# Windowed attention and feed-forward layer: half of the weight halves on GpSimd, the first token tile split straight from PSUM, the weight decode moved to later steps

## The chip, the cores and the metric

The kernel runs on one core of a Trainium2 chip. The metric is the device time of one execution in microseconds (us), as the median of several executions. A profiled execution gives the trace that is read below: the busy times of the engines TensorE (PE, with its weight loads as PEld), VectorE (DVE), ScalarE (ACT) and GpSimd (POOL), and of the DMA queue that SyncE (SP) issues.

## The reference

The kernel computes attention for 8 batches of 8 heads, with 512 local and 32 global tokens of 64 values each. A global token sees every token; a local token sees the 32 global tokens and the local ones within 32 places. The result, as 4352 rows of 512 values, goes through a feed-forward layer whose weights are given in 64 bit.

```python
s_g = scale * np.matmul(q_g, k_all.transpose(0, 1, 3, 2))
out_g = np.matmul(sm(s_g), v_all)
mask = np.abs(pos[:, None] - pos[None, :]) <= window          # window = 32
s_l = np.concatenate([s_lg, np.where(mask, s_ll, -1e9)], axis=-1)
out_l = np.matmul(sm(s_l), np.concatenate([v_g, v_l], axis=2))
...
h = x @ w_in            # (4352, 512) @ (512, 2048)
r = np.maximum(h, 0.0)
g = s * (r * r) + b
return (g @ w_out).astype(np.float32)
```

## The kernel before

**Steps.** One loop runs over steps j. Step j below 128 handles one slot of attention: batch, half of 256 queries, and head, in that order, so that eight steps fill one tile of 256 tokens by 512 values. Feed-forward unit m follows ten steps behind (LAG = 10): unit m works on tile t = m // 8 and on two of the 16 pieces of the hidden layer. It multiplies the tile with its two pieces of w_in (`ffn_in`, 24 matmuls, L517), squares and scales (L523 to L533), and one step later multiplies with two pieces of w_out (`ffn_out`, 12 matmuls, L549). Units 0 to 7 work on tile 0 and so need chunks 0 and 1, then 2 and 3, up to 14 and 15 of the weights, in steps 10 to 17.

**Precision.** Every operand of a fast matmul is split into a high half in the fp32r format and a low half, value minus high half; three products stand for one. The first 16 steps (NF = 16, tiles 0 and 1 of the tokens) instead use plain float32 matmuls for attention, which need no split of keys, queries and values.

**Weights.** A chunk holds 128 x 512 values of w_in and of w_out, each of 64 bits, 1 MB in all. `weight_load` brings it into a staging tile of the place that SPOTS names: xs0 or xs1 (the places that later hold the split token tiles) or one of two kq places (later the split keys and queries). `weight_chunk` decodes it in two halves, w_in first (`at.start` 0) and then w_out (`at.start` 512), in `weight_words`: two ACT operations (L160, L161), a shift and a sum on DVE (L164, L165), the high half on ACT (L168) and the low half on DVE (L169). DECODED_AT gives the step at which the decode of each chunk is issued in program order, here chunk k in step k; its load is issued two steps earlier.

**Token tiles.** In float32 steps `pv32` writes, at every odd head, a block of 128 x 256 values from PSUM to the tile x, with a DVE copy for the first eight steps (L349) and an ACT copy later (L347). One step after a tile is complete, `x_split` makes its high halves on ACT (L489) and its low halves on DVE (L490), two blocks of 128 x 512 each. SPLIT_AT names those steps: tile 0 in step 9.

**Order of the engines' queues.** The program order gives priorities only. A planner orders the instructions of every engine by priority, with a model of their durations, and an instruction is placed where its inputs and its place in memory are free in that model. Attention of the first 16 steps is given a priority 50 places earlier than its position (AHEAD = 50). On the chip every engine runs its own queue strictly in the planned order.

Of the kernel before, what the change touches and what calls it, by code (L numbers as in the profile page):

```python
# [23 lines left out]
HALF = 256  # L24
# [23 lines left out]
SPLIT_AT = {8 * t + 9: t for t in range(16)}  # L48
# [1 line left out]
WARM_FIRST = 20  # L50
WARM_HEAD = 4

SPOTS = ["xs0", "xs1", "kq", "kq"] * 2 + ["xs1", "kq", "kq"] * 2 + ["xs1", "kq"]
DECODED_AT = list(range(16))
BY_HALVES = 16
NORM_ACT = lambda j: j < 0
X_ACT = lambda j: j >= 8
# [8 lines left out]
def f32(ap):  # L66
    return ap.bitcast(F32)
# [3 lines left out]
def window_attention_then_ffn(ctx: ExitStack, tc: tile.TileContext, qd, qg, kw, vw, vg, qz, qgz, vz, w_in, w_out, sv, bv, out):  # L71
    nc = tc.nc
# [37 lines left out]
    for tile_, c0, shift in ((mask_low, 32, -32), (mask_mid, 32, 0), (mask_high, 0, 32)):  # L110
        nc.gpsimd.memset(tile_, 0.0)
        part = tile_[:, c0:c0 + 192]
        for sign, base in ((1, -shift), (-1, 64 + shift)):
            nc.gpsimd.affine_select(
                out=part, in_=part, pattern=[[sign, 192]], compare_op=ALU.is_ge,
# [16 lines left out]
    def split_tile(tag, name, shape, bufs):  # L132
        n = math.prod(shape)
        whole = ops.tile([P, n], F32R, tag=tag, name=name, bufs=bufs)
        return whole[:, 0:n].rearrange("p (a b c) -> p a b c", a=shape[0], b=shape[1])
# [3 lines left out]
    def weight_load(k):  # L139
        st = ops.tile([P, 2048], I32, tag=SPOTS[k], name=f"wst{k}", bufs=1 + (SPOTS[k] == "kq"))  # L140
        staged[k] = st
        sources = (w_in[k], w_out[k * P:(k + 1) * P, :])
        for i in range(2):
            queue = nc.scalar if k == 0 else nc.sync
            queue.dma_start(st[:, 1024 * i:1024 * (i + 1)], sources[i])

    def weight_chunk(k):
        st = staged.pop(k)
        n = 2 if k < BY_HALVES else 1
        for i in range(n):  # L150
            c = 1024 // n
            weight_words(k, st[:, 2 * c * i:2 * c * (i + 1)], slice(c * i, c * (i + 1)))

    def weight_words(k, st, at):
        words = st.rearrange("p (n w) -> p n w", w=2)
        low, high = words[:, :, 0], words[:, :, 1]
        n = at.stop - at.start
        pool, tag = ((ops, "vsg"), (sb, "pg"))[(k + at.start // 512) % 2]
        up = pool.tile([P, n], I32, tag=tag, name=f"wup{k}_{at.start}", bufs=1)
        nc.scalar.activation(out=up, in_=low.bitcast(U32), func=AF.Copy, scale=2.0**-29)  # L160
        nc.scalar.activation(  # L161
            out=low.bitcast(F32), in_=high.bitcast(F32), func=AF.Prelu, scale=2.0**-112, alpha=2.0**32,
        )
        nc.vector.tensor_scalar(out=low, in0=low, scalar1=3, scalar2=None, op0=ALU.logical_shift_left)  # L164
        nc.vector.tensor_tensor(out=low, in0=low, in1=up, op=ALU.add)  # L165
        m = low.bitcast(F32)
        hi, lo = (w_all[:, i, k].rearrange("p w c -> p (w c)")[:, at] for i in range(2))
        nc.scalar.copy(out=hi, in_=m)  # L168
        nc.vector.tensor_sub(out=lo, in0=m, in1=f32(hi))  # L169


    NS = B * 2 * H
# [2 lines left out]
    def slot(j):  # L175
        return j // 16, (j // 8) % 2, j % 8
# [77 lines left out]
    def x_tile(j):  # L254
        b, hf, h = slot(j)
        t = 2 * b + hf
        if h == 0:
            xcur[t] = sb.tile([P, 4, HALF], F32, tag="x", name=f"x{t}", bufs=1)
        return xcur[t]
# [56 lines left out]
    def pieces(hf):  # L316
        q0 = MIDQ[hf][0]
        yield 0, P, slice(0, P), slice(0, P)
        yield 2, P, slice(NP - P, NP), slice(P, 2 * P)
        yield 1, MID, slice(P, NP - P), slice(q0, q0 + NP - 2 * P)  # L320
# [10 lines left out]

    def pv32(j):
        b, hf, h = slot(j)
        x = x_tile(j)
        if h % 2 == 0:
            return
        p_o = ps.tile([P, 2 * P], F32, tag="o", name=f"ps_o{j}")
        for i in (j - 1, j):
            pt, rv = st_.pop(("pt", i)), st_.pop(("rv", i))
            for c, n, o, q in pieces(hf):  # L340
                nc.tensor.matmul(
                    p_o[:, q], lhsT=rv[0:n, c * P:(c + 1) * P], rhs=pt[0:n, o],
                    start=(i < j and c == 0), stop=(i == j and c == 1),
                )
        x_out = x[:, h // 2, :]
        if X_ACT(j):
            nc.scalar.copy(out=x_out, in_=p_o)  # L347
        else:
            nc.vector.tensor_copy(out=x_out, in_=p_o)  # L349

    def qg_load(b):
        rqg = sb.tile([P, H * SG], F32, tag="xr", name=f"rqg{b}", bufs=1)
        nc.sync.dma_start(rqg, qgz[0] if b == 0 else qg[b])
        st_["rqg", b] = rqg

    def qg_load32(b):
        n = min(NF - 16 * b, H) * SG
        rqg = ops.tile([P, n], F32, tag="u", name=f"rqw{b}", bufs=1)
        nc.sync.dma_start(rqg, qgz[b, :, 0:n])
        st_["rqg", b] = rqg  # L360

    def qg_split(b):
        rqg = st_["rqg", b].rearrange("p (h q) -> p h q", h=H)
        qgs = ops.tile([P, H, 2, SG], F32R, tag="qgs", name=f"qgs{b}", bufs=1)
        nc.scalar.copy(out=qgs[:, :, 0, :], in_=rqg)
        nc.gpsimd.tensor_sub(out=qgs[:, :, 1, :], in0=rqg, in1=f32(qgs[:, :, 0, :]))
        st_["qgs", b] = qgs
# [48 lines left out]
    def transposes_and_pv(jt, jp):  # L416
        if NF <= jp < NS:
            pv_products(jp)
        if NF <= jt < NS:
            p_transposes(jt)  # L420
        if NF <= jp < NS:
            pv_sum(jp)
        if NF <= jt < NS:
            p_split(jt)
# [57 lines left out]
    xs_ = {}  # L482
# [25 lines left out]
    def ffn_in(m):  # L508
        t, pr = m // 8, m % 8
        xs = xs_[t]  # L510
        p_h = ps.tile([P, 2, HALF], F32, tag="h", name=f"ps_h{m}", bufs=2)
        for k in range(2):
            f = 2 * pr + k
            n = 0
            for c in range(4):
                for a, e in ((0, 0), (0, 1), (1, 0)):
                    nc.tensor.matmul(  # L517
                        p_h[:, k], lhsT=wi[:, a, f, c], rhs=xs[:, e, c, :],
                        start=(n == 0), stop=(n == 11),
                    )  # L520
                    n += 1
        r = sb.tile([P, 2, HALF], F32, tag="r", name=f"r{m}", bufs=2)
        nc.scalar.activation(out=r, in_=p_h, func=AF.Relu)  # L523
        nc.vector.scalar_tensor_tensor(out=r, in0=p_h, scalar=s_t, in1=r, op0=ALU.mult, op1=ALU.mult)  # L524
        g = split_tile("g", f"g{m}", [2, 2, HALF], 2)
        if GL_POOL(m):
            nc.vector.tensor_scalar_add(r, r, b_t)
            nc.scalar.copy(out=g[:, 0], in_=r)
            nc.gpsimd.tensor_sub(out=g[:, 1], in0=r, in1=f32(g[:, 0]))
        else:  # L530
            nc.scalar.activation(out=g[:, 0], in_=r, func=AF.Identity, bias=b_t)  # L531
            nc.vector.scalar_tensor_tensor(  # L532
                out=g[:, 1], in0=r, scalar=b_t, in1=f32(g[:, 0]), op0=ALU.add, op1=ALU.subtract,  # L533
            )
        gs_[m] = g
# [32 lines left out]
    for b in range(B):  # L568
        for g in range(2):
# [4 lines left out]
            for i in range(2):  # L574
                h = 4 * g + 2 * i
# [23 lines left out]
    for j in range(NM + LAG + 2):  # L599
        if j == 3:  # L600
            nc.sync.dma_start(s_t, sv.partition_broadcast(P))
            nc.sync.dma_start(b_t, bv.partition_broadcast(P))
        sp(j + 1)
        ld(j + 2)
        vl(j)
        while loaded < 16 and (loaded < 2 or DECODED_AT[loaded] <= j + 2):
            weight_load(loaded)
            loaded += 1
        while piece < 16 and DECODED_AT[piece] <= j:
            weight_chunk(piece)  # L610
            piece += 1
        if j < NS:
            b1 = j // 16 + 1
            if j == 14 and NF > 16:
                qg_load32(1)
            elif j % 16 == 14 and b1 < B:
                qg_load(b1)
            sc(j)
            if j == NF - 1 and NF % 16:
                if NF > 16:  # L620
                    qg_load(j // 16)
                qg_split(j // 16)
            if j % 16 == 15 and NF <= j + 1 < NS:
                qg_split(b1)
        if j in early:
            early.pop(j)()
        m = j - LAG if LAG <= j < NM + LAG else None
        if m is not None:
            ffn_in(m)
            if m == 8 * 15 + 7:  # L630
                xg_split(16)
        tr(j - 1)
        transposes_and_pv(j - 1, j - 2)
        vsp(j - 1)
        for fn in extra.pop(j, []):
            fn()
        pvs(j - 2)
        vl32(j)
        if j in SPLIT_AT:
            x_split(SPLIT_AT[j])  # L640
        if last is not None:
            ffn_out(last)
        last = m
        if j in late:
            late.pop(j)()
# [73 lines left out]
```

## Time and profile before

| | us |
|---|---|
| median of 3 runs (1012.87 to 1013.37) | 1012.92 |
| the profiled execution | 1013.71 |
| its span in the trace | 1011.9 |
| PE / DVE / ACT / POOL busy within the span | 996.1 / 809.4 / 707.6 / 289.4 |
| first and last low half of a weight (L169) starts at | 8.4 / 103.6 |

The engines run side by side, and an engine's share of the whole span is an average over two stages: the first hundred us, in which the weights are decoded beside the float32 attention and the first feed-forward units, and the rest, in which nothing is decoded. A busy time of PE includes matmuls whose ends are modelled, so a busy PE isn't a PE at its peak. The chain of waits tells, for every stretch, on which engine the work ran that released the next.

### The profile page before, as it was taken

To read this page: it belongs to the slowest core of one execution; us is meant where nothing else is said; L and a number is where in the kernel's file an instruction comes from. 1 tells how busy PE (TensorE), PEld (TensorE's weight loads), DVE (VectorE), ACT (ScalarE), POOL (GpSimd) and SP (SyncE) were. 2 spreads that over 40 slices of the span, in tenths; PEclk is the share of its full clock that TensorE was granted. 3 is DMA by queue.
4 is the path that set the end of the run, shared out by engine and by line. 5 is a ranking of instruction groups with operands and counts; after the bars stand their busy time and mean duration, and the time that the engine had idled before them with its cause. 6 is when DMAs were issued, how large, how long until landed. Compare 5 with 4: busy or idle time off the path is not lost.

```text
span 1011.9 us, 20076 instructions
## 1 busy us (share of the span) xinstructions
PE 996.1 (98%) x6946; PEld 906.9 (90%) x6948; DVE 809.4 (80%) x2111; ACT 707.6 (70%) x1817; POOL 289.4 (29%) x366
## 2 busy tenths in 40 slices
PE   9799999999999999999999999999999999999998
PEld 5599899999999999999999999999999999999887
DVE  6999879988789788888789779988799788964322
ACT  7999767868677667868677667867678667743222
POOL 1001433424244224424234223424234223401000
PEclk9999999999999999999999999999999999999999
DMA  9765312313122212313132112312132112101000
GB/s 327 266 229 182 98 48 63 108 34 96 47 88 69 65 48 62 97 42 90 47 99 69 54 59 62 97 42 87 44 104 70 53 55 65 62 1 49 23 22 21
DMA packets 63557, 82.05 MB, mean 81 GB/s; under 512 B 7648, under 2 KB 50656, under 8 KB 63456
## 3 DMA queue, kind: packets, MB, share of 16 engines
q1 hardware_dynamic: 63168, 79.72, 25.2%
q8 instruction: 55, 0.90, 0.4%
q10 hardware_dynamic: 288, 1.05, 0.3%
q14 instruction: 46, 0.38, 0.1%
HBM read 71.30 MB, written 9.44 MB: 80 GB/s over the span
## 4 chain that ended last, share of the span: by engine, by line
PE 91%; ACT 5%; DVE 2%; DMA 1%; issue 0%
PE ps_h L517 35%; PE acc L549 35%; PE ps_s L375 5%; PE ps_o L403 4%; PE turned L311 3%; PE turned L313 3%; PE ps_og L469 2%; PE ps_g L382 1%; PE warm L105 1%; DMA rk<-in_kw 1%; ACT wst L161 1%; ACT wup L160 1%; ACT w_all L168 1%; ACT sm L231 1%; PE turned L447 1%; PE ps_s L286 1%
## 5 line engine op out<-in xcount | busy, mean ns | idle before, releaser
L517 PE MATMUL ps_h<-xst,w_all 128*128 128x256 f32 x3264 | 437.5, 281 | 1.8 <-ACT xst L502 0.7
L549 PE MATMUL acc<-w_all,g 128*128 128x512 f32 x1632 | 422.0, 396 | 0.0
L517 PEld LDWEIGHTS ps_h<-xst,w_all 128*128 128x128 f32 x3264 | 407.6, 189 | 9.3 <-ACT xst L489 1.1
L549 PEld LDWEIGHTS acc<-w_all,g 128*128 128x128 f32 x1632 | 289.8, 188 | 49.8
L214 POOL TENSOR_TENSOR vs<-rv,vs 128x192 fp32r<-128x192 f32 x112 | 70.7, 631 | 291.0 <-ACT vs L213 289.9
L524 DVE SCALAR_TENSOR_TENSOR r<-ps_h,s_t,r 128x512 f32<-128x512 f32 x136 | 101.4, 746 | 53.7 <-ACT r L523 52.2
L231 ACT ACTIVATE sm<-sm,nm 128x224 f32<-128x224 f32 x256 | 121.5, 478 | 32.5 <-DVE nm L225 31.3
L206 POOL TENSOR_TENSOR kq<-rq,kq 128x256 fp32r<-128x256 f32 x112 | 92.8, 828 | 169.2 <-ACT kq L205 160.3
L532 DVE SCALAR_TENSOR_TENSOR g<-r,b_t,g 128x512 fp32r<-128x512 f32 x136 | 112.0, 824 | 35.6 <-ACT g L531 31.1
L531 ACT ACTIVATE g<-r,b_t 128x512 fp32r<-128x512 f32 x136 | 98.6, 725 | 52.0 <-DVE r L524 51.9
L523 ACT ACTIVATE r<-ps_h 128x512 f32<-128x512 f32 x136 | 81.3, 598 | 67.7 <-PE ps_h L517 58.4
L241 DVE TENSOR_SCALAR sm<-sm,nm 128x224 f32<-128x224 f32 x256 | 92.2, 402 | 3.9
L461 POOL TENSOR_TENSOR vsg<-rvg,vsg 128x320 fp32r<-128x320 f32 x64 | 56.9, 910 | 107.1 <-ACT vsg L460 107.1
L375 PE MATMUL ps_s<-kq 128*128 128x224 f32 x448 | 73.7, 275 | 2.3 <-DVE nm L225 2.3
L375 PEld LDWEIGHTS ps_s<-kq 128*128 128x128 f32 x448 | 67.3, 190 | 8.9 <-ACT pt L328 2.5
L392 ACT CAST pt<-turned 128x416 fp32r<-128x416 f32 x112 | 57.5, 514 | 23.5 <-PE turned L313 22.8
L393 DVE TENSOR_TENSOR pt<-turned,pt 128x416 fp32r<-128x416 f32 x112 | 65.4, 584 | 6.9 <-ACT pt L392 6.2
L386 ACT COPY tg<-ps_g 32x256 f32<-32x256 f32 (+1 forms) x112 | 42.2, 377 | 33.9 <-PE ps_g L382 31.4
L387 DVE TENSOR_TENSOR sg<-ps_g,tg 32x256 f32<-32x256 f32 (+1 forms) x112 | 48.2, 430 | 20.7 <-ACT tg L386 15.9
L311 PE MATMUL turned<-ident,sm 128*96 128x128 f32 (+1 forms) x256 | 63.9, 274 | 0.0
L313 PE MATMUL turned<-ident,sm 128*128 128x128 f32 x256 | 63.2, 273 | 0.0
L403 PE MATMUL ps_o<-pt,vs 128*128 128x256 f32 x336 | 62.6, 295 | 0.0
(79 smaller groups left out, 1288.0 us busy)
## 6 DMA issues: line engine op xcount, KB each, us to landing
rq<-in_qd SPq DMA_DIRECT2D x112, 128.0 KB, 2.1
rk<-in_kw SPq DMA_DIRECT2D x64, 176.0 KB, 2.3
rv<-in_vw SPq DMA_DIRECT2D x112, 96.0 KB, 1.9
rvg<-in_vg SPq DMA_DIRECT2D x32, 320.0 KB, 3.0
out<-o SPq DMA_DIRECT2D x34, 256.0 KB, 2.2
wst<-in_w_in SPq DMA_DIRECT2D x15, 512.0 KB, 4.4
wst<-in_w_out SPq DMA_DIRECT2D x15, 512.0 KB, 5.5
rv<-in_vz SPq DMA_DIRECT2D x16, 192.0 KB, 4.2
```

What stands on the lines that cost most here:

```text
L206: nc.gpsimd.tensor_sub(out=qs[:, 1, :], in0=rq, in1=f32(qs[:, 0, :]))
L231: nc.scalar.activation(out=p, in_=p, func=AF.Exp, bias=nm[:, blk:blk + 1], scale=-1.0, accum_out=ss[:, blk:blk + 1],)
L241: nc.vector.tensor_scalar(out=p, in0=p, scalar1=ss[:, blk:blk + 1], scalar2=1.0, op0=ALU.mult, op1=ALU.mult,)
L311: nc.tensor.transpose(out=p_t[0:n, s0:s0 + P], in_=sm[:, c0:c0 + n], identity=ident)
L313: nc.tensor.transpose(out=p_t[:, o0:o0 + P], in_=sm[:, c0:c0 + P], identity=ident)
L375: nc.tensor.matmul(p_s[:, W * blk:W * blk + W], lhsT=qs[:, a, blk * P:(blk + 1) * P], rhs=ks[:, KEYS[blk]], start=(a == 0), stop=(a == 1),)
L403: nc.tensor.matmul(p_o[:, :, q], lhsT=vs[0:n, c], rhs=pt[0:n, :, o], start=(c == 0), stop=(c == 1))
L517: nc.tensor.matmul(p_h[:, k], lhsT=wi[:, a, f, c], rhs=xs[:, e, c, :], start=(n == 0), stop=(n == 11),)
L524: nc.vector.scalar_tensor_tensor(out=r, in0=p_h, scalar=s_t, in1=r, op0=ALU.mult, op1=ALU.mult)
L531: nc.scalar.activation(out=g[:, 0], in_=r, func=AF.Identity, bias=b_t)
L532: nc.vector.scalar_tensor_tensor(out=g[:, 1], in0=r, scalar=b_t, in1=f32(g[:, 0]), op0=ALU.add, op1=ALU.subtract,)
L549: nc.tensor.matmul(oacc[t][i], lhsT=g[:, a, k, i * P:(i + 1) * P], rhs=wo[:, e, f, :], start=(pr == 0 and n == 0), stop=(pr == 7 and n == 5),)
```

## The change

There are three parts. First, of the four high and low halves that each chunk needs, GpSimd makes two: the high half of w_in (before on ACT) and the low half of w_out (before on DVE). Second, tile 0 is no longer copied to x and split afterwards: in `pv32`, for the first eight steps, ACT rounds the block from PSUM straight to the high half, and DVE subtracts it from the same PSUM block to make the low half; `x_split` in step 9 falls away. Since the split tile 0 now lies in xs0 from the first steps on, xs0 no longer stages weights: chunks 0, 3, 6, 9, 12 and 15 go through xs1 and the other ten through the two kq places. Third, the steps of the decode are changed: six chunks in steps 1, 3, 5, 7, 8 and 9, and the ten others in steps 10 to 16.

```diff
-SPOTS = ["xs0", "xs1", "kq", "kq"] * 2 + ["xs1", "kq", "kq"] * 2 + ["xs1", "kq"]
-DECODED_AT = list(range(16))
+SPOTS = ['xs1', 'kq', 'kq', 'xs1', 'kq', 'kq', 'xs1', 'kq', 'kq', 'xs1', 'kq', 'kq', 'xs1', 'kq', 'kq', 'xs1']
+DECODED_AT = [1, 3, 5, 7, 8, 9, 10, 10, 11, 12, 12, 13, 14, 15, 15, 16]
...
         hi, lo = (w_all[:, i, k].rearrange("p w c -> p (w c)")[:, at] for i in range(2))
-        nc.scalar.copy(out=hi, in_=m)
-        nc.vector.tensor_sub(out=lo, in0=m, in1=f32(hi))
+        if not at.start:
+            nc.gpsimd.tensor_copy(out=hi, in_=m)
+        else:
+            nc.scalar.copy(out=hi, in_=m)
+        (nc.gpsimd if at.start else nc.vector).tensor_sub(out=lo, in0=m, in1=f32(hi))
...
-        x = x_tile(j)
+        x = x_tile(j) if j >= 8 else None
...
+        if j < 8:
+            if h == 1:
+                xs_[0] = split_tile("xs0", "xst0", [2, 4, HALF], 1)
+            hi, lo = (xs_[0][:, i, h // 2, :] for i in range(2))
+            nc.scalar.copy(out=hi, in_=p_o)
+            nc.vector.tensor_sub(out=lo, in0=p_o, in1=f32(hi))
+            return
...
-        if j in SPLIT_AT:
+        if SPLIT_AT.get(j, 0):
             x_split(SPLIT_AT[j])
```

## Rows read from the trace of the kernel before

**Rows 1.** The page, part 1: busy us, share of the span and instructions of each engine.

```profile
PE 996.1 (98%) x6946; PEld 906.9 (90%) x6948; DVE 809.4 (80%) x2111; ACT 707.6 (70%) x1817; POOL 289.4 (29%) x366
```

**Rows 2.** Busy time of each engine in five stretches: the stretch, its length, busy us of PE, PEld, DVE, ACT and POOL with their instructions, the granted share of TensorE's clock, the share of the DMA engines, GB/s.

```profile
0.00:10.00 10.00, 8.55 (x29) 3.65 (x29) 3.24 (x10) 4.87 (x8) 3.19 (x15) 1.00 0.83 296
10.00:50.00 40.00, 33.95 (x190) 23.77 (x192) 37.05 (x128) 39.27 (x99) 0.00 (x0) 1.00 0.86 299
50.00:104.00 54.00, 53.71 (x360) 48.84 (x359) 52.23 (x130) 53.33 (x119) 5.04 (x7) 1.00 0.58 194
104.00:120.00 16.00, 13.74 (x98) 12.86 (x98) 13.59 (x34) 11.78 (x33) 8.94 (x10) 0.89 0.31 91
120.00:240.00 120.00, 120.00 (x867) 111.58 (x866) 102.40 (x273) 87.75 (x234) 41.35 (x51) 1.00 0.24 73
```

**Rows 3.** The chain of waits from 46 to 118 us, in order of time: start, us on the chain, engine, tile and line.

```profile
50.46 0.51 ACT xst L489
50.97 0.57 ACT w_all L168
...
90.85 0.58 ACT wst L161
91.45 0.44 DVE wst L164
...
97.74 0.59 DVE w_all L169
...
107.42 0.30 DVE sm L225
...
107.88 0.68 PE ps_s L375 x4
```

**Rows 4.** Groups of instructions on DVE from 0 to 104 us: line, engine, operation, names, shapes and count, then busy us and mean ns of one, then idle time before them.

```profile
L165 DVE CUSTOM_DVE_ANT_0 wst<-wst,wup 128x1024 uint16<-128x1024 uint16 x32 | 22.7, 709 | 0.3
L169 DVE TENSOR_TENSOR w_all<-wst,w_all 128x512 fp32r<-128x512 f32 x32 | 22.3, 700 | 1.2 <-ACT w_all L168 0.9
L164 DVE TENSOR_SCALAR wst<-wst 128x512 int32<-128x512 int32 x32 | 13.6, 425 | 6.7 <-ACT wst L161 6.2
L241 DVE TENSOR_SCALAR sm<-sm,nm 128x224 f32<-128x224 f32 x32 | 9.4, 337 | 0.1
...
L532 DVE SCALAR_TENSOR_TENSOR g<-r,b_t,g 128x512 fp32r<-128x512 f32 x7 | 5.2, 748 | 0.4 <-ACT g L531 0.2
...
L490 DVE TENSOR_TENSOR xst<-x,xst 128x512 fp32r<-128x512 f32 x3 | 2.0, 683 | 0.0
L349 DVE COPY x<-ps_o 128x256 f32<-128x256 f32 x4 | 1.7, 418 | 0.8 <-PE ps_o L341 0.8
```

**Rows 5.** The same view of ACT from 0 to 104 us.

```profile
L168 ACT CAST w_all<-wst 128x512 fp32r<-128x512 f32 x32 | 21.3, 665 | 0.4 <-DVE wst L165 0.3
...
L489 ACT CAST xst<-x 128x512 fp32r<-128x512 f32 x3 | 1.8, 607 | 0.0
...
L347 ACT COPY x<-ps_o 128x256 f32<-128x256 f32 x3 | 1.1, 382 | 0.0
```

**Rows 6.** The same view of DVE over the whole span, for one line: a sum of a PSUM block and a tile, 128 x 256.

```profile
L411 DVE TENSOR_TENSOR u<-ps_o,u 128x256 f32<-128x256 f32 x112 | 46.4, 415 | 4.5 <-ACT u L410 4.5
```

**Rows 7.** The same view of POOL over the whole span: two subtractions with two inputs each, and two operations with one input.

```profile
L214 POOL TENSOR_TENSOR vs<-rv,vs 128x192 fp32r<-128x192 f32 x112 | 70.7, 631 | 291.0 <-ACT vs L213 289.9
...
L461 POOL TENSOR_TENSOR vsg<-rvg,vsg 128x320 fp32r<-128x320 f32 x64 | 56.9, 910 | 107.1 <-ACT vsg L460 107.1
...
L114 POOL TENSOR_SCALAR_AFFINE_SELECT mask_low<-mask_low 128x192 bf16<-128x192 bf16 x2 | 0.7, 346 | 0.0
...
masks.py:199 POOL TENSOR_SCALAR_AFFINE_SELECT ident<-ident 128x128 f32<-128x128 f32 x1 | 0.3, 292 | 0.0
```

**Rows 8.** Instructions in order of time around 95 us: start, us, engine, line, operation, names and shapes.

```profile
94.28 1.10 POOL L204 TENSOR_TENSOR kq<-rk,kq 64x352 fp32r<-64x352 f32 x1
94.61 1.32 DVE L165 CUSTOM_DVE_ANT_0 wst<-wst,wup 128x1024 uint16<-128x1024 uint16 x1
...
95.46 1.07 POOL L206 TENSOR_TENSOR kq<-rq,kq 128x256 fp32r<-128x256 f32 x1
...
95.86 1.22 DVE L169 TENSOR_TENSOR w_all<-wst,w_all 128x512 fp32r<-128x512 f32 x1
```

**Rows 9.** The same view from 104 to 107 us.

```profile
103.97 1.92 POOL L461 TENSOR_TENSOR vsg<-rvg,vsg 128x320 fp32r<-128x320 f32 x2 [0.68 <-ACT vsg L460]
104.22 1.81 DVE L241 TENSOR_SCALAR sm<-sm,nm 128x224 f32<-128x224 f32 x2
...
106.68 1.09 POOL L204 TENSOR_TENSOR kq<-rk,kq 64x352 fp32r<-64x352 f32 x1
107.02 0.39 DVE L225 CUSTOM_DVE_ANT_0 sm<-ps_s,mask_low 128x224 f32<-128x224 f32 x1
```

**Rows 10.** The issues of the weight loads on SP's queue in order of time, the loads of w_in of chunks 9, 12 and 15, which use the same kind of place: start, us of the issue, queue and line.

```profile
51.19 0.33 SPq L145 DMA_DIRECT2D wst<-in_w_in  x1
...
71.69 0.33 SPq L145 DMA_DIRECT2D wst<-in_w_in  x1
...
87.56 0.33 SPq L145 DMA_DIRECT2D wst<-in_w_in  x1
```

**Rows 11.** The chain of waits from 0 to 50 us, in the same columns as rows 3.

```profile
22.02 8.20 DMA rk<-in_kw
...
43.17 2.27 DMA rk<-in_kw
```

## The prediction

> **What bounds the kernel now.** I read the shares of the page first. PE is busy for 98% of the span, DVE for 80%, ACT for 70%, POOL for 29% [rows 1]. That average hides two stages, which the table by stretches separates [rows 2]. From 120 us on PE has no idle time and DVE and ACT have slack (102.40 and 87.75 of 120 us); nothing that the change touches lies there. From 10 to 104 us, the stage of the decode, ACT is busy for 39.27 + 53.33 = 92.6 of 94 us and DVE for 37.05 + 52.23 = 89.3. POOL does 5.04 us in that time. So in the stage that is changed two engines are full, and the third that could help is empty. Third, the chain of waits says which of the full ones ends last: it runs over ACT from 50 to 91 us, over DVE from 91 to 107, and only from 107.88 us over PE [rows 3]. A microsecond taken from both DVE and ACT before 107 us comes off the total; taken from one alone, it is worth the slack of the other. DVE's slack from 10 to 104 us is 94 - 89.3 = 4.7 us, ACT's is 1.4.
>
> My sum therefore goes over DVE's work before 104 us, since DVE is the engine on which the change both takes and adds. ACT only gains.
>
> **First part: two of four halves to GpSimd.** ACT loses 16 of the 32 high halves. One takes 665 ns [rows 5], on the chain 0.57 us from one start to the next [rows 3]: 16 x 0.57 = 9.1 us off ACT. DVE loses 16 of the 32 low halves, 0.59 us each on the chain [rows 3]: 16 x 0.59 = 9.4 us off DVE.
>
> GpSimd gains 16 copies and 16 subtractions of 128x512, neither of which the trace shows. The subtraction: 128x192 takes 631 ns and 128x320 takes 910 [rows 7], 2.18 ns a column, so 910 + 192 x 2.18 = 1.33 us. The copy has one input. Its nearest rows are the two selections, 292 ns for 128 columns and 346 for 192 [rows 7], 0.84 ns a column, so 346 + 320 x 0.84 = 0.62 us; at most it costs what two inputs cost, 1.33. I take 0.62, the row of the same kind. GpSimd's own work is 16 x 1.95 = 31.2 us in some 100 us in which it was idle, which by itself would hide.
>
> It doesn't hide from DVE. At 94.28 us POOL begins an operation that ends at 95.38; DVE's L165, begun at 94.61, takes 1.32 us where the mean is 0.71; the next low half takes 1.22 beside the next POOL operation [rows 8, 4]. Two L241 take 1.81 us beside L461, and L225, which reads PSUM, takes its usual 0.39 beside L204 [rows 9]. So a DVE instruction with two inputs in SBUF, or a scaling from SBUF to SBUF, stands until POOL is done: L165 had 0.77 us left of POOL's operation and lost about 0.63, all but 0.14. What reads PSUM goes on.
>
> The blocked lines are L165 (22.7 us), half of L169 (11.2), L164 (13.6, no row of it beside POOL, taken as blocked because L241 is an operation of the same kind), L241 (9.4) and L532 (5.2) [rows 4], 62 us. DVE's work to 104 us is 3.24 + 37.05 + 52.23 = 92.5 [rows 2], after the change about 81. Neighbouring instructions overlap a little, so I put the share at 0.7 and not at 62/81 = 0.76. The loss is 0.7 x (31.2 - 32 x 0.14) = 0.7 x 26.7 = 18.7 us. From below: around 95 and 105 us the three delays shown, 0.6 + 0.5 + 1.15 = 2.3 us, stand against 1.10 + 1.07 + 1.92 + 1.09 = 5.2 us of POOL, 0.44 a microsecond; if moreover the copy with its one input blocks nothing, the loss is 0.44 x 16 x 1.33 = 9.4 us, my lower end. From above: everything blocked, 26.7.
>
> The Trainium skill, "SBUF — State Buffer", section "SBUF: two separate sides", speaks against this part: VectorE and GpSimd share a pair of ports that one instruction holds to its end, and the other blocks fully instead of sharing. The rows agree except for the last 0.14 us; by the page's whole duration the loss would be 0.7 x 31.2 = 21.8 us and the sum below 3.1 us higher.
>
> **Second part: tile 0 from PSUM.** DVE loses four copies of 418 ns and two subtractions of 683 [rows 4], 3.0 us, and gains four subtractions that read PSUM, each like L411 with 415 ns [rows 6], 1.7 us: 1.3 us off. ACT loses two roundings of 607 ns and gains four like L347 with 382 [rows 5], 0.3 us more. The PSUM block is held one operation longer, 0.4 us, which the two steps between such blocks hide.
>
> **Third part: later decode.** No work is added. Attention of steps 0 to 9 has less decode before it in the queues, and unit 0 of the feed-forward layer, whose tile was split up to 51 us [rows 3], can begin sooner. The ten chunks left then meet the feed-forward units: the work moves within a stage in which DVE is full throughout, so I cost it at nothing. That cover is gone if DVE isn't the bound. Of the moved loads each is two issues on SP's queue of 0.33 to 0.4 us [rows 10]; behind them stand the loads of keys, queries and values. Now one key load lands 8.20 us after its issue, and a later one 2.27 [rows 11], so up to 5.9 us can be won there, if nothing else then ends last. A new wait is that of DVE's low half of w_in on GpSimd's copy, where it waited on ACT before. Behind it in DVE's queue stand the masks and scalings of the softmax, and PE waits for those.
>
> **The sum.** DVE: -9.4 - 1.3 + 18.7 = +8.0 us. ACT's relief lets DVE fill its slack, at most 4.7 us. Left: +3.3 us, on the profiled execution 1013.71 + 3.3 = 1017.0 (span 1011.9 to about 1015.2). That execution is 0.8 us above the median of the runs, so I predict 1012.92 + 3.3 = 1016.2.
>
> **The rivals.** *ACT was the bound* (chance 0.35). For it: the chain runs 41 us on ACT without a break, and DVE has the larger slack. If DVE's loss is near the lower end, 9.4 to 12, its sum is -1.3 to +1.3, well inside the slack of 4.7, and ACT's relief counts: 9.1 - 0.3 = 8.8 us at most, of which the early 8.20 us landing and PE's own work leave some two thirds. That gives 1004 to 1009, middle 1007. Against it: in 91 to 107 us, where DVE ends last, the only POOL work so far already delays it. It decides below a loss of about 0.5 us a microsecond of POOL: 0.5 x 31.2 - 9.4 - 1.3 = 4.9, about the slack.
>
> *The two cancel* (0.20): loss between 14 and 17 us, 1011 to 1015.
>
> *The staging places become the bound* (0.12). A kind of place is loaded again 20.5 us and then 15.9 us after its last load [rows 10], each time when its decode is done; with three places and none in xs0 that is 5.3 us a chunk at best. GpSimd's subtraction ends each decode 1.33 - 0.70 = 0.6 us later, the copy and the turn at the ports another 1.4, 2 us in all, 0.7 a chunk over ten chunks: 6.7 us, 1020. The point from which it decides is a place held longer than three times what the engines need for a chunk, some 16 us. The full blocking of 26.7 us ends in the same region, up to 1024.
>
> *The change doesn't do what it says*: the planner pulls the decode forward again whenever a place is free, so that the third part does nothing. Since I cost it at nothing, my time stays.
>
> **Chances and range.** Forecast 0.33, ACT's rival 0.35 spread over six microseconds, cancelling 0.20, staging 0.12. Each of the two largest is about as likely; that the sum from the rows comes out above zero, and that DVE ends last where the decode ends, let me take the forecast as the single time. A measurement of this kernel tells 0.2%, about 2 us, from no change. Faster than 1010.9: 0.35. Within: 0.20. Slower than 1014.9: 0.45. The range goes from 1005 to 1022, leaving out the best of ACT's rival and the full blocking.
>
> **What would show it.** Right: L165, L164 and L241 with means well above 0.71, 0.43 and 0.34 before the last low half; POOL busy for 30 to 40 us more; DVE with almost no idle time and ACT with 8 us or more of it; the chain on DVE from 50 us on; the last low half at 106 us or later. Wrong: these means unchanged, which takes away the 18.7; the last low half before 100 us; the chain still on ACT, which makes the first rival true; a POOL copy over 1 us or SP waiting for places longer than 16 us, which points to the third.

## The result and the profile after

The changed kernel takes 1019.07 us in the median of four runs (1018.59 to 1019.33), beside 1013.14 for the kernel before (1012.87 to 1013.64). The ratio is 1.0052 with a 95% interval of 1.004 to 1.0065, so it is 4.1 to 6.6 us slower. The profiled execution took 1019.2 us with a span of 1017.4, against 1013.71 and 1011.9.

The page of the changed kernel, part 1, answers to [rows 1]:

```profile
PE 1000.2 (98%) x6948; PEld 907.0 (89%) x6948; DVE 816.7 (80%) x2093; ACT 700.3 (69%) x1803; POOL 325.0 (32%) x398
```

POOL has 35.6 us more to do and ACT 7.3 less. DVE, which was to be relieved, has 7.3 us more. The stretches say where, against [rows 2]:

```profile
0.00:10.00 10.00, 8.08 (x29) 3.52 (x30) 3.02 (x8) 4.47 (x7) 3.83 (x16) 1.00 0.85 293
10.00:50.00 40.00, 36.08 (x200) 24.59 (x199) 37.27 (x118) 36.28 (x94) 13.67 (x13) 1.00 0.85 294
50.00:104.00 54.00, 49.65 (x325) 43.96 (x324) 53.49 (x114) 47.99 (x104) 23.52 (x23) 1.00 0.59 195
104.00:120.00 16.00, 14.54 (x89) 12.86 (x89) 15.51 (x36) 12.16 (x34) 11.85 (x12) 0.79 0.34 99
120.00:240.00 120.00, 119.91 (x854) 110.59 (x853) 99.46 (x267) 83.85 (x226) 39.87 (x51) 1.00 0.22 66
```

From 10 to 104 us ACT's idle time grew from 1.4 to 94 - 84.3 = 9.7 us, while DVE's shrank from 4.7 to 94 - 90.8 = 3.2 us. DVE is the full engine now, and from 50 to 104 us it has half a microsecond left. From 120 us on PE is full in both kernels, and nothing of the change lies there.

The groups on DVE up to the last low half (0 to 112 us) answer to [rows 4]; L244 is the old L241, L172 the old L169, L542 the old L532, and L237 the small sum that was L234:

```profile
L165 DVE CUSTOM_DVE_ANT_0 wst<-wst,wup 128x1024 uint16<-128x1024 uint16 x32 | 23.9, 750 | 0.4
L244 DVE TENSOR_SCALAR sm<-sm,nm 128x224 f32<-128x224 f32 x34 | 19.2, 601 | 0.2
L164 DVE TENSOR_SCALAR wst<-wst 128x512 int32<-128x512 int32 x32 | 15.3, 480 | 6.0 <-ACT wst L161 6.0
L172 DVE TENSOR_TENSOR w_all<-wst,w_all 128x512 fp32r<-128x512 f32 x16 | 12.9, 804 | 0.0
L542 DVE SCALAR_TENSOR_TENSOR g<-r,b_t,g 128x512 fp32r<-128x512 f32 x7 | 7.1, 1017 | 0.0
...
L237 DVE TENSOR_SCALAR nm<-nm 128x2 f32<-128x2 f32 x17 | 6.8, 401 | 2.2 <-ACT sm L234 2.2
L534 DVE SCALAR_TENSOR_TENSOR r<-ps_h,s_t,r 128x512 f32<-128x512 f32 x7 | 5.2, 741 | 0.0
...
L238 DVE RECIPROCAL nm<-nm 128x2 f32<-128x2 f32 x17 | 2.7, 160 | 0.3
```

The small operations and the line that reads PSUM, in the kernel before (0 to 104 us):

```profile
L524 DVE SCALAR_TENSOR_TENSOR r<-ps_h,s_t,r 128x512 f32<-128x512 f32 x7 | 5.2, 743 | 0.1
...
L234 DVE TENSOR_SCALAR nm<-nm 128x2 f32<-128x2 f32 x17 | 2.8, 163 | 0.9 <-ACT sm L231 0.7
L235 DVE RECIPROCAL nm<-nm 128x2 f32<-128x2 f32 x17 | 2.7, 159 | 0.2
```

Same instructions, longer means. Against the means before, the six lines lost (750 - 709) x 32 + (601 - 337) x 34 + (480 - 425) x 32 + (804 - 700) x 16 + (1017 - 748) x 7 + (401 - 163) x 17 ns = 1.31 + 8.98 + 1.76 + 1.66 + 1.88 + 4.05 = 19.6 us. The scaling of the softmax (L244) lost most: 13 of its 34 begin while GpSimd is at work, against 5 of the 32 of L165. An operation on two columns (L237) was held up no less than one on 512. The line that reads PSUM (L534, the old L524) and the reciprocals (L238, the old L235) kept their means.

In order of time, one such place of the changed kernel:

```profile
85.60 1.72 POOL L172 TENSOR_TENSOR w_all<-wst,w_all 128x512 fp32r<-128x512 f32 x1 [2.36 <-ACT w_all L171]
...
86.25 1.84 DVE L244 TENSOR_SCALAR sm<-sm,nm 128x224 f32<-128x224 f32 x2
87.27 0.69 POOL L169 CAST w_all<-wst 128x512 fp32r<-128x512 f32 x1
...
88.02 1.23 DVE L542 SCALAR_TENSOR_TENSOR g<-r,b_t,g 128x512 fp32r<-128x512 f32 x1
```

On POOL's own line the operation behind that copy is:

```profile
87.92 0.78 POOL L376 TENSOR_TENSOR qgs<-rqg,qgs 128x256 fp32r<-128x256 f32 x1
```

A subtraction holds POOL from 85.60 to 87.32 and the copy until 87.96; DVE's pair of scalings, begun at 86.25 and worth 0.65 us, ends at 88.09. The next DVE operation, normally 0.75 us, is 1.23 long: it stands beside a subtraction of the attention (L376, until 88.70), which is no part of the change.

The chain of waits of the changed kernel, in the columns of [rows 3]:

```profile
75.51 0.50 ACT r L533
76.01 0.43 DVE wst L164
...
86.25 1.84 DVE sm L244 x2
88.10 1.15 DVE g L542
...
94.81 1.74 DVE g L542
96.55 1.47 DVE wst L164
...
101.15 1.42 DVE w_all L172
102.59 0.49 ACT kq L206
```

From 76 to 102.6 us it runs over DVE, but for waits of under a microsecond that the profile doesn't explain. Its long pieces are instructions that wait for GpSimd. From 46 to 76 us it is mixed, with DVE, PE, ACT and two waits for loads of queries (4.33 us from 47.58 and 3.94 from 60.33). Before the change the chain was on ACT until 91, and not quite "without a break", as the prediction has it: 1.8 us at 65 were DVE's.

What PE does with the loss is seen in its matmuls by stretch (columns: the stretch, its length, busy us and instructions of PE, of PEld, clock, DMA). Those of `ffn_in` and `ffn_out` before:

```profile
0.00:50.00 50.00, 1.95 (x12) 1.56 (x12) 1.00 0.86 299
50.00:90.00 40.00, 18.76 (x132) 16.76 (x132) 1.00 0.68 228
90.00:120.00 30.00, 12.58 (x88) 11.54 (x89) 0.94 0.30 95
```

```profile
50.00:90.00 40.00, 14.60 (x58) 10.42 (x59) 1.00 0.68 228
90.00:120.00 30.00, 10.50 (x40) 7.01 (x38) 0.94 0.30 95
```

and after:

```profile
0.00:50.00 50.00, 5.26 (x26) 3.72 (x27) 1.00 0.85 294
50.00:90.00 40.00, 17.03 (x120) 14.75 (x119) 1.00 0.69 226
90.00:120.00 30.00, 12.16 (x78) 10.40 (x79) 0.89 0.33 102
```

```profile
50.00:90.00 40.00, 14.44 (x55) 10.04 (x56) 1.00 0.69 226
90.00:120.00 30.00, 9.43 (x31) 6.32 (x29) 0.89 0.33 102
```

Up to 50 us the changed kernel is ahead: 26 matmuls of `ffn_in` where 12 were done. From 50 to 120 us it does 22 of `ffn_in` and 12 of `ffn_out` fewer. On the chain of the kernel before, after 136 us, 19 matmuls of L517 take 2.17 us and 12 of L549 take 2.73, so that is 22 x 0.114 + 12 x 0.228 - 14 x 0.114 = 3.6 us of feed-forward work behind at 120 us. Over all matmuls, by the stretches above, it is 643 against 677 by 120 us and 1497 against 1544 by 240 us; at the 867 in 120 us of the kernel before, being behind by 34 and 47 is worth an estimated 4.7 and 6.5 us, which fits the loss measured. PE's busy time shows little of it (109.95 us before and 108.35 after, up to 120 us), since the ends of matmuls are modelled.

### The profile page after: what moved, and what is told of

Same layout as the page of the kernel before. It is cut to its first block, busy times and chain, and to the rows that moved or that the text cites. A ratio compares the mean times of both kernels' runs of the same rounds, so it can differ in the third digit from the quotient of the medians.

```text
span 1017.4 us, 20133 instructions
## 1 busy us (share of the span) xinstructions
PE 1000.2 (98%) x6948; PEld 907.0 (89%) x6948; DVE 816.7 (80%) x2093; ACT 700.3 (69%) x1803; POOL 325.0 (32%) x398
## 4 chain that ended last, share of the span: by engine, by line
PE 86%; DVE 7%; ACT 3%; DMA 2%; issue 1%; SPq 0%; ACTq 0%; DVEq 0%
PE acc L559 34%; PE ps_h L527 34%; PE ps_s L385 5%; PE ps_o L413 4%; PE turned L314 2%; PE turned L316 2%; PE ps_og L479 2%; DMA wst<-in_w_out 1%; PE ps_g L392 1%; DVE sm L244 1%; DVE wst L165 1%; DVE wst L164 1%; PE turned L457 1%; DMA rq<-in_qz 1%; DVE w_all L172 1%
## 5 line engine op out<-in xcount | busy, mean ns | idle before, releaser
L234 ACT ACTIVATE sm<-sm,nm 128x224 f32<-128x224 f32 x256 | 121.6, 478 | 34.3 <-DVE nm L228 33.0
L542 DVE SCALAR_TENSOR_TENSOR g<-r,b_t,g 128x512 fp32r<-128x512 f32 x136 | 113.0, 831 | 38.9 <-ACT g L541 34.4
L534 DVE SCALAR_TENSOR_TENSOR r<-ps_h,s_t,r 128x512 f32<-128x512 f32 x136 | 101.4, 746 | 52.5 <-ACT r L533 51.4
L244 DVE TENSOR_SCALAR sm<-sm,nm 128x224 f32<-128x224 f32 x256 | 100.6, 434 | 4.1
```

What stands on the lines that cost most here:

```text
L234: nc.scalar.activation(out=p, in_=p, func=AF.Exp, bias=nm[:, blk:blk + 1], scale=-1.0, accum_out=ss[:, blk:blk + 1],)
L244: nc.vector.tensor_scalar(out=p, in0=p, scalar1=ss[:, blk:blk + 1], scalar2=1.0, op0=ALU.mult, op1=ALU.mult,)
L542: nc.vector.scalar_tensor_tensor(out=g[:, 1], in0=r, scalar=b_t, in1=f32(g[:, 0]), op0=ALU.add, op1=ALU.subtract,)
```

## The experiments

All ratios are to the kernel before on the same chip, with 95% intervals; a us is given at 1013 us.

**1. The first part alone.** Halves on GpSimd; places, steps and split of tile 0 as before.

```diff
-        nc.scalar.copy(out=hi, in_=m)
-        nc.vector.tensor_sub(out=lo, in0=m, in1=f32(hi))
+        if not at.start:
+            nc.gpsimd.tensor_copy(out=hi, in_=m)
+        else:
+            nc.scalar.copy(out=hi, in_=m)
+        (nc.gpsimd if at.start else nc.vector).tensor_sub(out=lo, in0=m, in1=f32(hi))
```

> Only the first part of the change: two of four halves on GpSimd, places, steps and the split of tile 0 as before. Blocking theory (GpSimd's operations hold up DVE, and DVE is what ends last): DVE loses 16 to 20 us to waits and sheds 9.4, so 3 to 8 us slower than before, 1016 to 1021. Steps theory (the later decode and the three staging places cost the time): within 2 us of before or faster, since only ACT and DVE shed work.

Measured: 1.0065 (1.0052 to 1.0078), 6.6 us slower. The first part alone costs as much as the whole change or a little more. The steps theory falls for this part. In its trace the same six lines lost 17.8 us, and DVE kept 2.05 us idle from 10 to 50 us and 0.44 from 50 to 104, so that it filled 2.2 of its 4.7: 17.8 - 9.4 - 2.2 = 6.2 us.

**2. The second and third part without the first.** The changed kernel with the two lines of the halves as before.

> The second and third part without the first: all halves on ACT and DVE as before, tile 0 from PSUM, xs0 without staging, the new steps. Blocking theory: no added GpSimd work, DVE sheds 1.3 us, so 0 to 3 us faster than before, 1010 to 1013. Steps theory: still 3 to 7 us slower than before, 1016 to 1020.

Measured: 1.0018 (1.0009 to 1.0027), 1.8 us slower. Neither theory had it: no loss of 3 us, but no gain either, though DVE sheds work and no added GpSimd work holds it up. Something in the second or third part costs.

**3. GpSimd work that nobody reads.** The kernel before with 48 subtractions added.

```diff
         nc.vector.tensor_sub(out=lo, in0=m, in1=f32(hi))
+        for i in range(2 if at.start else 1):
+            idle = const.tile([P, 232], F32, tag="idle", name=f"idle{k}_{at.start}_{i}", bufs=1)
+            nc.gpsimd.tensor_sub(out=idle, in0=f32(hi)[:, 0:232], in1=f32(hi)[:, 256:488])
```

> The kernel before with 48 GpSimd subtractions of 128x232 added, three per chunk behind its high halves, whose result nobody reads: some 33 us of GpSimd work and nothing taken from ACT or DVE. Blocking theory: DVE loses some 0.6 us for each us of GpSimd work, 18 to 20 us, less its 4.7 us of slack: 1024 to 1029. If GpSimd's work cost only through those who wait for its results (rival): within 2 us of before.

Measured: 1.0119 (1.0103 to 1.0135), 12.1 us slower, for work whose result no one waits for. The rival falls. The groups on DVE of this kernel, 0 to 118 us:

```profile
L165 DVE CUSTOM_DVE_ANT_0 wst<-wst,wup 128x1024 uint16<-128x1024 uint16 x32 | 25.6, 800 | 0.2
L169 DVE TENSOR_TENSOR w_all<-wst,w_all 128x512 fp32r<-128x512 f32 x32 | 24.2, 757 | 0.7 <-ACT w_all L168 0.7
L164 DVE TENSOR_SCALAR wst<-wst 128x512 int32<-128x512 int32 x32 | 17.2, 540 | 5.3 <-ACT wst L161 5.2
L244 DVE TENSOR_SCALAR sm<-sm,nm 128x224 f32<-128x224 f32 x33 | 14.5, 479 | 0.1
```

and the added work on POOL:

```profile
L172 POOL TENSOR_TENSOR idle<-w_all 128x232 f32<-128x232 f32 x47 | 42.0, 894 | 64.6 <-ACT w_all L168 62.6
```

The lines that lost in the changed kernel lose here as well, L164 among them, which the trace of before had not shown beside POOL. The time is in the lower half of what was expected: these four lost (91 x 32 + 57 x 32 + 115 x 32 + 142 x 33) ns = 13.1 us, where 18 to 20 had been put down for all lines together. GpSimd's work was 42.0 us and not the 33 expected, so a microsecond of it cost less: with three smaller lines (3.2 us) DVE lost 16.3 us, 0.39 us a us. Another order of DVE's instructions isn't what costs. The first 196 stand in the same order as in the kernel before; they take 85.3 us in place of 75.2, and the last of them begins at 80.64 us where it began at 72.02.

**4. The old steps in the changed kernel.** DECODED_AT as before, all else as changed.

> The changed kernel with the steps of the decode as before, chunk k in step k; halves on GpSimd, places and split of tile 0 as changed. Blocking theory: the work is the same and DVE is full either way, so within 3 us of the changed kernel, 1016 to 1022. Steps theory: most of the loss is gone, 1011 to 1015.

Measured: 1.0042 (1.0025 to 1.0058). With 1.0052 (1.004 to 1.0065) for the whole change the intervals overlap: the later steps bring and cost nothing that can be told.

**5. The second part alone.** The kernel of experiment 2 with DECODED_AT as before.

> The second part alone: tile 0 from PSUM, with the places that it asks for, the old steps of the decode and no halves on GpSimd. If the later steps cost the 1.8 us of the run with the second and third part, this one is at or under the kernel before: 0 to 2 us faster. If the places do (xs0 lost for staging), it is 1 to 3 us slower than before, like that run.

Measured: 1.0041 (1.0028 to 1.0053), 4.2 us slower, on the side of the places. From 10 to 50 and from 50 to 104 us of this kernel:

```profile
10.00:50.00 40.00, 36.34 (x189) 25.84 (x190) 33.27 (x116) 36.41 (x95) 0.00 (x0) 0.91 0.80 271
50.00:104.00 54.00, 50.59 (x333) 45.84 (x332) 50.54 (x131) 52.65 (x118) 5.17 (x6) 0.98 0.67 219
```

Early, ACT idles 3.6 us where it idled 0.7, and DVE 6.7 where it idled 3.0: they have less decode to work on; the loads come later, as experiment 9 shows.

**6. Only the copies on GpSimd.**

```diff
-        (nc.gpsimd if at.start else nc.vector).tensor_sub(out=lo, in0=m, in1=f32(hi))
+        nc.vector.tensor_sub(out=lo, in0=m, in1=f32(hi))
```

> The changed kernel with only the 16 copies on GpSimd; the low halves of w_out are back on DVE. GpSimd's added work is 12.6 us in place of 35.8. Blocking theory: DVE loses 0.47 us per us of it, 6 us, and sheds nothing against the run without GpSimd halves, but ACT sheds 9: 0 to 4 us slower than that run, so 1015 to 1020 where before is 1014. If the copy with its single input doesn't hold DVE up: 1 to 5 us faster than that run.

Measured: 1.0034 (1.0022 to 1.0045), 1.6 us slower than experiment 2, within the range of the blocking theory, but the intervals of the two overlap (2.2 to 4.6 us here, 0.9 to 2.7 there). The trace says more than the time. A copy has one input and blocks all the same, in order of time:

```profile
65.57 1.04 POOL L169 CAST w_all<-wst 128x512 fp32r<-128x512 f32 x1 [0.91 <-DVE wst L165]
66.03 0.14 DVE L442 TENSOR_SCALAR gm<-gm 128x1 f32<-128x1 f32 x1
66.09 0.81 DVE L164 TENSOR_SCALAR wst<-wst 128x512 int32<-128x512 int32 x1
```

L164, else 0.43 us, ends 0.29 us after the copy (66.90 and 66.61). The operation on one column (L442) in front of it, beside the same copy, isn't held.

**7. Only the subtractions on GpSimd.**

```diff
-        if not at.start:
-            nc.gpsimd.tensor_copy(out=hi, in_=m)
-        else:
-            nc.scalar.copy(out=hi, in_=m)
+        nc.scalar.copy(out=hi, in_=m)
```

> The changed kernel with only the 16 subtractions on GpSimd; the high halves of w_in are back on ACT. GpSimd's added work is 23.2 us. Blocking theory: DVE loses 11 us and sheds 9.4, ACT sheds nothing: 2 to 6 us slower than the run without GpSimd halves, 1017 to 1022 where before is 1014. If a subtraction moved to an idle engine is worth its 0.59 us on DVE: faster than that run by 2 us or more.

Measured: 1.0092 (1.0079 to 1.0105), 9.3 us slower, 7.5 more than experiment 2. The sign is that of the blocking theory, the size above its range. The stretch from 50 to 104 us is not that of a full DVE:

```profile
50.00:104.00 54.00, 47.89 (x318) 42.76 (x316) 48.28 (x110) 50.84 (x110) 17.58 (x15) 0.99 0.62 206
```

DVE idles 5.7 us and ACT 3.2, so waits between the engines were added to DVE's. The chain of waits of this run shows one of them:

```profile
87.57 1.46 POOL w_all L169
...
89.05 0.33 SPq L145
...
89.43 4.82 DMA wst<-in_w_out
```

From 61.8 to 89 us it follows the subtractions on GpSimd, with long waits between them that the profile doesn't explain. A weight load is issued at 89.05, when a subtraction ends, and the decode waits for it. This is the way in which the prediction's staging rival was to cost; in the changed kernel ACT and DVE wait for no weight load from 50 us on. How much of the 9.3 us it makes wasn't tested; that the copies, added to this kernel, make it faster again (9.3 to 5.3 us) stays without a cause that was shown.

**8. A remedy: scaling on ACT.** NORM_ACT for the even float32 steps, in the changed kernel.

```diff
-NORM_ACT = lambda j: j < 0
+NORM_ACT = lambda j: j < 16 and j % 2 == 0
```

> The changed kernel with the scaling of the softmax of the eight even float32 steps on ACT in place of DVE. It is the DVE work that loses most beside GpSimd. Blocking theory: DVE sheds 16 times 0.33 us and about 4 us of waiting, 9 us, ACT takes on some 7 us and has 8 to spare: 4 to 9 us faster than the changed kernel, 1010 to 1015 where before is 1014. If ACT or the staging places set the end: no faster than the changed kernel, 1018 to 1024.

Measured: 1.0071 (1.0054 to 1.0087): no faster, the expectation of the blocking theory missed. From 50 to 104 us:

```profile
50.00:104.00 54.00, 51.15 (x342) 46.65 (x341) 50.41 (x114) 52.27 (x119) 24.90 (x24) 1.00 0.64 211
```

DVE has 3.6 us of idle time again (and 8.0 from 10 to 50 us, where it does 31.95 us of work) and ACT 1.7: the relief of DVE is there, but the end didn't come sooner. The chain of waits of this run lies on PE, from here

```profile
50.83 3.23 PE ps_h L527 x26
```

to 94 us, and on DVE only from 96 to 110. So DVE's work alone doesn't set the time: with DVE relieved, PE ends last in the middle of the stage. Why the whole is then no faster stays open.

**9. The places alone.** SPOTS as changed, in the kernel before.

> The kernel before with only the places of the staging changed as in the change (xs0 no longer used, chunks 0, 3, 6, 9, 12, 15 in xs1). Places theory (the second part costs because the first four chunks can't all be loaded at once any more): 2 to 5 us slower than before, the load of chunk 3 at 12 us or later where it is 8.5 now, and 2 us or more of new idle time on ACT between 10 and 50 us. If the split from PSUM is what costs in the second part: within 2 us of before.

Measured: 1.0039 (1.0025 to 1.0053), 4.0 us slower, in the range of the places theory. The load of chunk 3 in order of time, in this kernel:

```profile
14.14 1.28 SPq L145 DMA_DIRECT2D wst<-in_w_in  x1
```

It was issued at 8.53 us in the kernel before. The load of chunk 4 comes at 22.59 us in place of 16.71. ACT's idle time from 10 to 50 us in the profiled execution is 1.6 us, under the 2 that were asked for; that execution, at 1015.76 us, was the fastest of its five.

**10. The later steps alone.** DECODED_AT as changed, in the kernel before.

> The kernel before with only the steps of the decode changed as in the change. If the later steps are worth the 2.4 us that lie between the two runs with and without them: 1 to 4 us faster than before, 1009 to 1012 where before is 1013. If what they move is full on DVE and ACT either way: within 2 us.

Measured: 0.9999 (0.999 to 1.0008). The third part alone is worth nothing, as the prediction costed it; the 2.4 us between experiments 2 and 5 arise only where the first chunks have three places. Here the load of chunk 3 is issued at 12.17 us and that of chunk 4 at 16.83, and nothing is lost, so a late load of chunk 3 is not by itself what costs in experiments 5 and 9.

**11. Half the delay.**

```diff
-DECODED_AT = list(range(16))
+DECODED_AT = [0, 1, 3, 4, 5, 7, 8, 9, 10, 11, 12, 12, 13, 14, 15, 15]
```

> The kernel before with the decode moved by at most two steps (0, 1, 3, 4, 5, 7, 8, 9, 10, 11, 12, 12, 13, 14, 15, 15). It asks whether an effect of the later steps grows with the delay or is the accident of one planned order: between before and the run with the full delay if it grows, anywhere within 4 us of before if it is the order.

Measured: 1.0004 (0.9995 to 1.0012). With experiment 10 there is no effect of the steps to grow, and the planned order, changed in both, moved the time by less than 1.2 us.

**12. The fourth place given back.** The kernel of experiment 5, chunks 0 and 4 staged in the two buffers of g.

```diff
-SPOTS = ['xs1', 'kq', 'kq', 'xs1', 'kq', 'kq', 'xs1', ...
+SPOTS = ["g", "xs1", "kq", "kq"] * 2 + ["xs1", "kq", "kq"] * 2 + ["xs1", "kq"]
...
+        if SPOTS[k] == "g":
+            st = [ops.tile([P, 1024], I32, tag="g", name=f"wst{k}_{i}", bufs=2) for i in range(2)]
```

> The run with the second part alone, with a fourth early place given back: chunks 0 and 4 staged in the two buffers of g, which the feed-forward units use only later. Places theory: the load of chunk 3 goes back to some 8.5 us and the 4.1 us of that run go away but for the 1.3 us that the split from PSUM takes off DVE: 0 to 2 us faster than before, 1011 to 1014 where before is 1013 to 1014. If the order that the planner makes, and not the places, cost the 4.1 us: anywhere between 1 us faster and 5 us slower than before.

Measured: 1.0006 (0.9997 to 1.0015), where experiment 5 had 1.0041. The load of chunk 3 is back:

```profile
8.49 0.67 SPq L149 DMA_DIRECT2D wst<-in_w_in  x1
```

3.5 of the 4.2 us go away with the place (the load of chunk 4 is issued at 10.63 us). Of the 1.3 us that the split from PSUM takes off DVE nothing shows; experiments 5 and 9, with and without that split, agree too. No version was faster than the kernel before by more than the noise.

## Why the prediction was right, and where not

**What held.** The direction, and the mechanism of the first part. GpSimd's operations stop DVE, shown by experiment 3, which takes no work from any engine and keeps the order of DVE's first 196 instructions. The loss on DVE was put at 18.7 us and read as 19.6. By the whole duration that "SBUF — State Buffer" of the Trainium skill states in "SBUF: two separate sides" the prediction's estimate was 21.8; the rows lie between. Most of the signs named for it came: POOL did 35.6 us more, ACT idled 9.7 us, and the last low half began at 109.3 us where it began at 103.6. L244's mean rose well (337 to 601 ns), L165's and L164's only by 41 and 55 ns, and the chain lay on DVE from 76 us on and not from 50.

**Terms of the first part.** GpSimd's work was estimated at 31.2 us and is 23.2 + 12.6 = 35.8, in which its own waits for DVE are counted (without them 16 x 1.94 = 31.0):

```profile
L172 POOL TENSOR_TENSOR w_all<-wst,w_all 128x512 fp32r<-128x512 f32 x16 | 23.2, 1454 | 34.5 <-ACT w_all L171 34.5
L169 POOL CAST w_all<-wst 128x512 fp32r<-128x512 f32 x16 | 12.6, 785 | 27.8 <-DVE wst L165 22.9 <-DVE nm L238 3.0 <-DMA rq<-in_qz 1.8
```

The shortest subtraction took 1.30 us and the shortest copy 0.64, beside 1.33 and 0.62. L237 was left out of the blocked lines and lost 4.0 us; the other five lost 15.6. So the loss of 18.7 us was met with two errors that offset each other: more GpSimd work (35.8 us) at a lower price (19.6 / 35.8 = 0.55 us a us, where 18.7 / 31.2 = 0.60 was put). By the prediction's own terms the first part alone is 18.7 - 9.4 - 4.7 = +4.6 us; it measured 6.6 (5.3 to 7.9). The slack was the term that was too large: I let DVE fill all its 4.7 us, and it kept 3.2 of them in the changed kernel and 2.5 in experiment 1. Most of what it kept lies before 50 us, and there 2.2 us of it in the changed kernel are L237's waits for ACT.

**The step that failed.** The second part, put at "1.3 us off" by its arithmetic alone, with no price for the staging place that it takes. It costs 4.2 us when it is alone: it takes the fourth staging place from the first chunks. I had named the places, as a rival for the late chunks; experiments 9 and 12 put the loss at the places of the first ones. Which load carries it stays open: with three places the loads of chunks 3 and 4 both come 5 to 6 us later, and in experiment 10 that of chunk 3 alone is late, by 3.6 us, at no cost. With halves on GpSimd this loss doesn't add: 6.6 for the one, 4.2 for the other, 5.3 (4.1 to 6.6) for all. The stretches fit a reason, that the lack of early chunks is hidden when DVE is held up anyway (33.27 us of work from 10 to 50 us in experiment 5, 37.27 in the changed kernel); it was not tested alone. So the sum of 3.3 us came near the measured 5.3 in part by luck: the first part was put too low, the second below nothing, and the two, added as measured alone, would make 10.8.

**The rivals.** ACT was not the bound once it was relieved: it idled 9.7 us and the time went up. The two didn't cancel. The staging rival's time, 1020 us, lies nearer to the measured 1019.07 than my 1016.2, but not by its mechanism: the places cost with the first chunks, and a wait for a late place shows on the chain of experiment 7 and not in the changed kernel. That the planner undoes the later steps didn't come true (in experiment 10 the load of chunk 3 moves from 8.53 to 12.17 us), and the third part made no difference all the same. TensorE's granted clock, which I hadn't named, doesn't explain the losses: its mean is 0.998 in experiment 1 and 0.999 in the runs of before beside it, and 0.996 in experiments 5, 9 and 12 alike (0.998 to 0.999 before), of which 12 loses 0.6 us and the others 4. It may carry a part of those 4.

## What to carry to other kernels

An engine that is idle is not free if it shares something with the full one: before work is moved to GpSimd, count which of VectorE's instructions would stand beside it, and set GpSimd's duration against the VectorE time that it saves. Here 1.3 us of GpSimd replaced 0.6 us of VectorE, and each microsecond of GpSimd held VectorE up for 0.55. A place in memory that a later tile takes early is a cost of its own: look at which transfers came later without that place, and give another one back before the parts are judged together; parts that each cost several microseconds may cost no more in sum than one of them.

## What the hardware showed unexpectedly

A copy on GpSimd with a single input (0.64 us for 128x512 alone) holds DVE up like a subtraction. The hold doesn't grow with what DVE's own instruction moves: a sum on 128x2 values had a mean of 0.40 us in place of 0.16. But the same kind of operation on 128x1 values (L442, 0.14 us beside the copy of experiment 6) was not held, nor were reciprocals on 128x2 values (L238, 160 ns; L235 before, 159) and the line that reads PSUM (L534, 741 ns; L524 before, 743).
